# Token-mixed rows transposed by sixteen SBUF-to-SBUF copies and VectorE blocks instead of TensorE, with scores two units ahead

## Chip, cores and metric

One core of one Trainium2 chip. The metric is the device time of one execution in microseconds (us), median of several. Profiles are of one execution each; where the record gives both, its span is 1.7 to 1.9 us shorter than its time. An *issue* below is the time that an engine's queue (SyncE's is `SPq`) is occupied with starting one DMA; a DMA *lands* when its data have arrived. SBUF is the memory of the kernel's tiles, PSUM that of the matmuls' results.

## The reference

Eight batches of pooled-key attention, then an MLP mixer on the result; all inputs and the output are float32, the kernel computes in bfloat16.

```python
# q, k, v: (8, 8, 576, 64); keys and values averaged over groups of 8 -> 72 keys
attn = softmax(q @ k_pooled^T / 8)            # per batch and head
x  = (attn @ v_pooled) as (batch, 576, 512)
h  = relu(x^T @ w_tok1) @ w_tok2              # token mixing: 576 -> 256 -> 576
u  = x + h^T
out = u + relu(u @ w_ch1) @ w_ch2             # channel MLP: 512 -> 1536 -> 512
```

The channel MLP's first matmul sums over the 512 channels, so `u`, made with tokens on the partitions, is needed transposed (`uT`, channels on the partitions).

## The kernel before

A *unit* is one batch's channel MLP: 48 matmuls of 512 columns in a first stage (w_ch1) and 48 in a second (w_ch2). Between them, at numbered steps (two matmuls each), stand the attention and token mixing of the next batch. The order on TensorE, GpSimd, VectorE (DVE) and ScalarE (ACT) is the order in which the program issues; the timelines keep to it (in unit 3 of the changed kernel VectorE stands 11.17 us before a block transpose, with a q block and a kD copy of 0.27 us behind it). The transpose and the schedule, cut:

```python
def uT(c):                                     # 4 TensorE transposes, then one VectorE copy from PSUM
    def go():
        src = st["u"][:, c, :] if c < 4 else u_tails[:, b // 2, :]
        ...
        for kk in range(4):
            nc.tensor.transpose(out=ps[:, kk, :], in_=src[:, kk * P:(kk + 1) * P], identity=ident)
        nc.vector.tensor_copy(out=dst[:, :, o:o + P], in_=ps)
...
TAIL = {23: "av0", 25: "av1", 27: "av2", 29: "av3", 31: "av4", 33: "at0", 34: "at1",
        37: "u0", 38: "u1", 39: "t0", 40: "u2", 41: "t1", 42: "u3", 43: "u4 t2", 45: "t3", 47: "t4"}
LATER = {0: "kpT", 3: "s0", 6: "P0", 8: "s1", 11: "P1", 13: "s2", 16: "P2", 18: "s3", 20: "P3", **TAIL}
```

`kpT` transposes the pooled keys (into `kD`), `Q`/`P` are VectorE's block transposes of q (into `qD`), `s` scores, `av` attention times values, `at` and `u` the token mixing, `t` the transposes of u. The last 64 of a batch's 576 rows go, two batches together, through a ninth unit (`u4`, `t4`, "tails").

The softmax here doesn't subtract the row's maximum and nothing guards it: scores larger than these inputs give would overflow.

## Time and profile before

| | before |
|---|---|
| time, median | 290.4 us (3 runs) |
| span of the profile | 290.8 us (of an execution of 292.6 us) |
| TensorE busy | 95% |
| VectorE / ScalarE / GpSimd busy | 52% / 33% / 45% |
| mean granted TensorE clock | 0.994 |
| TensorE holes over 0.5 us after the start-up | unit 0 and its end only, but for two of 0.6 us at unit boundaries |

"Busy" counts overlapping matmuls once, so I read TensorE by the distances of its starts: 216 ns for 512 columns. A *hole* below is the distance of two neighbouring starts less that pace. The lines are in the prediction.

### The profile page before, as it was taken

To read this page: it belongs to the slowest core of one execution; us is meant where nothing else is said; L and a number is where in the kernel's file an instruction comes from. 1 tells how busy PE (TensorE), PEld (TensorE's weight loads), DVE (VectorE), ACT (ScalarE), POOL (GpSimd) and SP (SyncE) were. 2 spreads that over 40 slices of the span, in tenths; PEclk is the share of its full clock that TensorE was granted. 3 is DMA by queue.
4 is the path that set the end of the run, shared out by engine and by line. 5 is a ranking of instruction groups with operands and counts; after the bars stand their busy time and mean duration, and the time that the engine had idled before them with its cause. 6 is when DMAs were issued, how large, how long until landed. Compare 5 with 4: busy or idle time off the path is not lost.

```text
span 290.8 us, 4636 instructions
## 1 busy us (share of the span) xinstructions
PE 276.8 (95%) x1876; PEld 137.9 (47%) x1912; DVE 151.3 (52%) x304; ACT 95.6 (33%) x173; POOL 130.1 (45%) x121
## 2 busy tenths in 40 slices
PE   7989989989999999999999999999999999999994
PEld 3755456433455445443544454445443545444443
DVE  5465814695377436754755476637551656121122
ACT  2544682004800470037103710173027200511500
POOL 8593103999999979940999934000000000000000
PEclk9999999997999999999999999999999999999999
DMA  7999999948829839552843011300320031114014
GB/s 150 194 205 205 204 195 187 229 82 132 152 42 158 191 39 177 111 86 61 146 92 72 2 32 42 72 0 2 72 60 14 2 73 41 34 36 102 6 38 108
DMA packets 25157, 27.97 MB, mean 96 GB/s; under 512 B 4656, under 2 KB 18864, under 8 KB 25136
## 3 DMA queue, kind: packets, MB, share of 16 engines
q0 software_dynamic: 18928, 17.64, 39.1%
q1 hardware_dynamic: 6048, 9.90, 14.1%
q8 instruction: 15, 0.25, 0.3%
q10 hardware_dynamic: 160, 0.13, 0.2%
q14 instruction: 6, 0.05, 0.1%
HBM read 35.85 MB, written 9.44 MB: 156 GB/s over the span
## 4 chain that ended last, share of the span: by engine, by line
PE 77%; POOL 10%; DVE 6%; ACT 2%; DMA 2%; issue 2%; POOLq 0%
PE p L473 26%; PE p L447 26%; PE p L387 5%; PE p L372 5%; POOL t L154 4%; PE p L326 3%; POOL t L155 3%; PE p L288 2%; PE pt L397 2%; DMA kr<-in_k_dram 2%; PE p L254 1%; PE p L306 1%; POOL kp L158 1%; DVE qD L277 1%; PE p L462 1%
## 5 line engine op out<-in xcount | busy, mean ns | idle before, releaser
L473 PE MATMUL p<-w_ch,GT 128*128 128x512 bf16 x401 | 105.8, 379 | 0.6
L447 PE MATMUL p<-uT,w_ch 128*128 128x512 bf16 x372 | 91.1, 383 | 0.9 <-issue 0.5
L452 ACT ACTIVATE GT<-p 128x512 bf16<-128x512 f32 x84 | 48.7, 596 | 108.2 <-PE p L447 95.9
L447 PEld LDWEIGHTS <-w_ch 128*128 128x128 bf16 x432 | 39.8, 98 | 47.2 <-issue 6.6
L473 PEld LDWEIGHTS <-GT 128*128 128x128 bf16 x420 | 37.5, 98 | 33.6 <-issue 0.2
L454 DVE TENSOR_SCALAR GT<-p 128x512 bf16<-128x512 f32 x24 | 16.6, 692 | 63.8 <-PE p L447 63.8
L155 POOL TENSOR_TENSOR t<-t 72x512 f32<-72x512 f32 x24 | 30.3, 1261 | 1.9
L294 ACT ACTIVATE ex<-p 72x576 bf16<-72x576 f32 x48 | 28.3, 640 | 6.6 <-PE p L288 6.6
L478 DVE TENSOR_TENSOR o<-p,u 128x512 f32<-128x512 f32 x32 | 22.0, 687 | 10.4 <-PE p L473 10.2
L388 DVE TENSOR_TENSOR u<-p,x 128x512 bf16<-128x512 f32 x32 | 22.1, 690 | 9.0 <-PE p L387 9.0
L154 POOL TENSOR_TENSOR t<-kr 72x1024 f32<-72x1024 bf16 x12 | 25.5, 2125 | 0.1
L154 POOL TENSOR_TENSOR t<-vr 72x1024 f32<-72x1024 bf16 x12 | 25.4, 2119 | 0.0
L363 ACT ACTIVATE AT<-p 128x512 bf16<-128x512 f32 x8 | 4.8, 597 | 52.8 <-PE p L372 50.1
L344 DVE TENSOR_TENSOR x<-p,den 128x512 bf16<-128x512 f32 x30 | 20.7, 692 | 1.0
L326 PEld LDWEIGHTS <-ex 72*128 72x128 bf16 x320 | 15.4, 98 | 9.9 <-DVE x L344 0.8
L387 PE MATMUL p<-AT,w_tok 128*128 128x512 bf16 x64 | 19.0, 379 | 0.1
L277 DVE STREAM_TRANSPOSE qD<-qb 128x576 bf16<-128x576 bf16 x24 | 18.7, 805 | 0.0
L326 PE MATMUL p<-vp,ex 72*128 72x65 bf16 x320 | 16.8, 194 | 0.9 <-DVE x L344 0.6
L365 DVE TENSOR_SCALAR AT<-p 128x512 bf16<-128x512 f32 x8 | 5.5, 692 | 17.3 <-PE p L372 16.5
L372 PE MATMUL p<-x,w_tok 128*128 128x512 bf16 x56 | 14.4, 379 | 0.1
L398 DVE COPY uT<-pt 128x512 bf16<-128x512 bf16 x28 | 11.8, 420 | 3.4 <-PE pt L397 3.4
L118 POOL DMA_DIRECT2D qb<-in_q_dram x6 | 4.3, 722 | 18.8 <-DVE qD L277 12.3
(93 smaller groups left out, 236.6 us busy)
## 6 DMA issues: line engine op xcount, KB each, us to landing
out_dram<-o SPq DMA_DIRECT2D x70, 128.0 KB, 2.4
kr<-in_k_dram POOLq DMA_DIRECT2D x7, 576.0 KB, 8.3
qb<-in_q_dram POOLq DMA_DIRECT2D x7, 576.0 KB, 10.5
vr<-in_v_dram POOLq DMA_DIRECT2D x7, 576.0 KB, 14.2
w_ch<-in_moe_w_ch_dram POOLq DMA_DIRECT2D x6, 512.0 KB, 12.8
qf<-in_q_dram SPq DMA_DIRECT2D x2, 288.0 KB, 3.0
kr<-in_k_dram POOLq DMA_DIRECT2D x2, 256.0 KB, 6.3
vr<-in_v_dram POOLq DMA_DIRECT2D x2, 256.0 KB, 7.6
```

The source lines that it names most:

```text
L154: eng.tensor_tensor(out=t4[:, 0:n], in0=t[:, hs, 0:4], in1=t[:, hs, 4:8], op=ALU.add)
L155: eng.tensor_tensor(out=t4[:, 0:n, 0:2], in0=t4[:, 0:n, 0:2], in1=t4[:, 0:n, 2:4], op=ALU.add)
L277: nc.vector.transpose(out=st["qD"][:, g, db].rearrange("m (r j u) -> m u r j", u=2, r=BR), in_=st["qraw"][:, g].rearrange("m (u r d) -> m ...
L294: nc.scalar.activation(out=exv[:, h:h + 2], in_=pss[a][0:SP, :, 0:SH], func=AF.Exp, scale=scale)
L326: nc.tensor.matmul(out=halves[h // 4][:, (h % 4) * (D + 1):(h % 4 + 1) * (D + 1)], lhsT=st["ex"][:, h * S + n0:h * S + n0 + P], rhs=st["vp ...
L372: nc.tensor.matmul(out=ps, lhsT=w_tok1[:, c if c < 4 else 4 + par, m * P:(m + 1) * P], rhs=st["x"][:, c, :] if c < 4 else st["xt"], start= ...
L387: nc.tensor.matmul(out=ps, lhsT=w, rhs=a, start=(i == 0), stop=(i == len(mms) - 1))
L388: nc.vector.tensor_tensor(out=dst, in0=ps, in1=x, op=ALU.add)
L447: nc.tensor.matmul(out=ps, lhsT=w_ch1[:, kk, m * P:(m + 1) * P], rhs=uT[:, kk, :], start=(kk == 0), stop=(kk == 3))
L452: nc.scalar.activation(out=GT[:, m, :], in_=ps, func=AF.Relu)
L473: nc.tensor.matmul(out=ps, lhsT=GT[:, m, c * P:(c + 1) * P], rhs=w_ch2[:, m, :], start=(m == 0), stop=(m == NM - 1))
L478: nc.vector.tensor_tensor(out=o_sb, in0=ps, in1=u_all[:, c, :], op=ALU.add)
```

## The change

The intent is to take the transposes of u off TensorE for batches 2 to 7. A 128x128 transpose is put together from sixteen copies, each of which moves a 32-partition quadrant to another quadrant, and from VectorE's transposes, which the program takes to work within blocks of 32x32. So that the score phase does not compete with ScalarE's activations in the first stage, scores are computed two batches ahead, in the second stage, and ScalarE takes all activations. w_ch1's rows are permuted to match. Batch 1 loses its special path.

```diff
+        def shuffle(part, src):
+            def go():
+                st[part] = swap.tile([P, 4 if part == "v" else 1, DM], BF16, name=part)
+                for a in range(4):
+                    for i in range(4):
+                        nc.sync.dma_start(out=st[part][32 * a:32 * a + 32, :, i * P:(i + 1) * P],
+                                          in_=src()[32 * i:32 * i + 32, :, a * P:(a + 1) * P])
...
+        def blocks(c):
+            def go():
...
+                nc.vector.transpose(out=dst[:, :, o:o + P].rearrange("f k (a t) -> f a k t", a=4),
+                                    in_=src.rearrange("t (a f k) -> t a k f", a=4, k=4))
...
-            if m % 4 != 3 or n == 0:
-                nc.scalar.activation(out=GT[:, m, :], in_=ps, func=AF.Relu)
-            else:
-                nc.vector.tensor_scalar(out=GT[:, m, :], in0=ps, scalar1=0.0, scalar2=None, op0=ALU.max)
+            nc.scalar.activation(out=GT[:, m, :], in_=ps, func=AF.Relu)
...
-    LATER = {0: "kpT", 3: "s0", 6: "P0", 8: "s1", 11: "P1", 13: "s2", 16: "P2", 18: "s3", 20: "P3", **TAIL}
+    FIRST = {0: "K0 V0", 1: "<u0", 2: "<u1", 4: "<u2", 6: "<u3 k1", 8: "Q0", 10: "Q1", 12: "kpT Q2", 14: "Q3 v1",
...
+    SECOND = {0: "s0 V0 V1 L >K0 >K1 >V0 >V1", 3: "s1", 6: "s2", 9: "s3", 13: "av0", 15: "av1", 17: "av2", 19: "av3", 21: "av4",
+              23: "at0 >Q0", 24: "at1", 27: "u0", 28: "u1", 30: "u2", 31: "u3 M", 33: "u4 M4 >Q1 >kpT", 34: "T0",
+              35: ">Q2", 36: "T1 >s0", 37: ">Q3", 38: "T2", 39: ">s1", 40: "T3", 42: "T4 >s2", 45: ">s3"}
+    LATER = {0: ">K0 >K1 L >V0 >V1 av0", 2: "av1", 4: "av2", 6: "av3", 8: "av4", 10: "at0 >Q0", 11: "at1",
+             14: "u0", 15: "u1", 17: "u2", 18: "u3 M", 20: "u4 M4 >Q1", 21: "T0", 22: "T1", 24: ">Q2 >kpT",
+             25: "T2", 27: ">Q3 >s0", 29: "T3", 31: "T4 >s1", 35: ">s2", 39: ">s3"}
```

`M` is the sixteen copies (`M4` those of the tails), `T` a block transpose, `>` marks work for the batch two ahead, `L` the loads of a batch three ahead, `K`/`V` GpSimd's pooling, `k`/`v` VectorE's. FIRST is unit 0, SECOND unit 1, LATER all others.

## The prediction

What no trace of this case shows is cut out of the recorded text, and the cuts are marked. After the first of them "what that is" means the issue of a DMA, after the second "such a VectorE operation" is a block transpose. One term of the sum is cut: +0.4 us for batch 1's scores in part 2. The trace before does not show it: there 16 score matmuls of the old form hold TensorE 2.0 us, 32 of the new form 1.5 us. The net of 2.5 us contains that term (without it 2.9), and the sum stands: 290.4 - 6.0 - 2.5 - 2 = 279.9 us, with 57.6 us of holes and 10.2 us of slow stretches 348 us, from which 341 us was chosen. A slow stretch of 1.7 us at each hole was the estimate, from the start-up's eight matmuls in 3.59 us.

> **What bounds the kernel now.** I read the busy table first, then the chain that ended last, then the costliest groups, then stretches of the timeline.
>
> ```profile
> PE 276.8 (95%) x1876; PEld 137.9 (47%) x1912; DVE 151.3 (52%) x304; ACT 95.6 (33%) x173; POOL 130.1 (45%) x121
> ...
> PE   7989989989999999999999999999999999999994
> ...
> PE 77%; POOL 10%; DVE 6%; ACT 2%; DMA 2%; issue 2%; POOLq 0%
> ```
>
> TensorE is busy 95% of the span, at 9 in nearly every slice, and the chain of waits runs on it for 77%. So the program is a queue of matmuls without holes, and a change pays only by what it takes out of that queue, or costs what it puts holes into it. The cadence of the queue is seen in the PE timeline of a stretch in the middle:
>
> ```profile
> 150.32 0.39 PE L397 MATMUL pt<-ident,u 128*128 128x128 bf16 x4
> 150.54 0.59 PE L473 MATMUL p<-w_ch,GT 128*128 128x512 bf16 x2
> 150.98 0.59 PE L387 MATMUL p<-AT,w_tok 128*128 128x512 bf16 x2
> ```
>
> The durations overlap (the matmuls are pipelined), so I take the distances of the starts: four transposes hold the queue 0.22 us (56 ns each), two 512-column matmuls 0.44 us (216 ns each). The groups name what the change removes:
>
> ```profile
> L397 PE MATMUL pt<-ident,u 128*128 128x128 bf16 x112 | 10.8, 219 | 0.2
> ...
> L397 PE MATMUL pt<-ident,u_tails 128*128 128x128 bf16 x16 | 1.5, 219 | 0.5 <-DVE uT L398 0.5
> ```
>
> 128 transposes look like 12.3 us of busy time there, but at 56 ns each they hold the queue only 7.2 us. The only real holes lie in the first batch's unit and at its end, in the PE timeline there:
>
> ```profile
> 63.64 0.38 PE L397 MATMUL pt<-ident,u_tails 128*128 128x128 bf16 x4 [0.46 <-DVE uT L398]
> ...
> 65.93 0.29 PE L215 MATMUL pt<-ident,kp 72*128 72x72 bf16 x4 [1.48 <-DVE uT_tails L398]
> ...
> 66.71 1.91 PE L447 MATMUL p<-uT,w_ch 128*128 128x512 bf16 x4 [0.22 <-issue]
> ```
>
> After that hole of some 1.5 us, four matmuls take 1.91 us, twice their usual pace. A hole costs itself and then a slow stretch. At the program's start (the PE timeline's first line) eight go in 3.59 us before the fast pace begins; against 8 x 216 ns = 1.7 us, some 1.7 us are lost.
>
> [...] The trace shows what that is in time, in SyncE's own timeline of two stretches:
>
> ```profile
> 0.74 0.86 SPq L108 DMA_DIRECT2D qf<-in_q_dram  x2
> ...
> 112.63 1.11 SPq L481 DMA_DIRECT2D out_dram<-o  x2
> ```
>
> that is 0.43 and 0.56 us per issue. [...] The trace has such a VectorE operation for q:
>
> ```profile
> L277 DVE STREAM_TRANSPOSE qD<-qb 128x576 bf16<-128x576 bf16 x24 | 18.7, 805 | 0.0
> ...
> L388 DVE TENSOR_TENSOR u<-p,x 128x512 bf16<-128x512 f32 x32 | 22.1, 690 | 9.0 <-PE p L387 9.0
> ...
> out_dram<-o SPq DMA_DIRECT2D x70, 128.0 KB, 2.4
> ```
>
> **The change, part by part.** A "unit" is one batch's channel MLP with the attention of later batches between its matmuls.
>
> 1. Removed from TensorE: of the 128 transposes of u, the built program keeps 20 (batch 1). 108 x 56 ns = 6.0 us, all on the path.
> 2. Batch 1 loses 20 q transposes (1.1 us), half of its v pooling on TensorE (16 matmuls of 256 columns, 109 ns apart, 1.7 us) and four small k transposes (0.1 us)[...]. Net 2.5 us.
> 3. Batch 1's pooling, before wholly a VectorE chain of some 5 us on which TensorE waits, is split with GpSimd. I allow 2 us for smaller holes in the first two units.
> 4. ScalarE takes all hidden activations (24 more of 596 ns) and the scores move to the second stage. ScalarE is 33% busy, so this costs nothing.
> 5. Added: for each of six batches, sixteen SBUF-to-SBUF DMAs of 32 KB, all issued by SyncE, then four VectorE block transposes; for odd batches sixteen further DMAs of 8 KB for the tail rows. VectorE loses the copies from PSUM (420 ns) and gets 512-element block transposes, estimated 805 x 512/576 = 0.72 us; with 52% busy that is affordable.
>
> Parts 1 to 3: 290.4 - 6.0 - 2.5 - 2 = 279.9 us without new holes.
>
> **Where part 5 puts holes.** I read the order of the built program. In units 2 to 5 TensorE has, between the last matmul of u3 (which the copies wait for) and the first score matmul of the batch two ahead, 18 matmuls of 216 ns and four small k transposes: 4.0 us, or 4.9 us in even units with the four tail matmuls. VectorE has in its queue: u3, one q block, first block transpose (waits for all sixteen copies), second one, another q block, and only then the copy of the k transposes that those scores need. So the scores wait for the copies, although they use nothing of them. The chain from the end of u3's matmul:
>
> - u3's addition with its latency: 0.9 us (0.69 + 0.2)
> - sixteen issues at 0.56 us: 8.9 us
> - landing of the last: 2.4 us from issue to landing, less its own issue: 1.8 us
> - two block transposes, a q block, the k copy (286 ns), latencies: 0.72 + 0.72 + 0.81 + 0.29 + 0.2 = 2.7 us
>
> Sum 14.3 us, so TensorE stands still 14.3 - 4.0 = 10.3 us in units 3 and 5 and 9.4 us in units 2 and 4. Unit 1 copies later, but its third score waits behind the first block transpose: 11.6 us to landing, plus 3.7 us of VectorE work, less 6.0 us of matmuls up to there, is 9.5 us with latency. Unit 6 has no scores ahead, but the tail's block transpose waits for 32 issues (20.5 us), and the additions that free the PSUM buffers stand behind it: 22.1 us against 13.4 us of matmuls, 8.7 us. Total 2 x 10.3 + 2 x 9.4 + 9.5 + 8.7 = 57.6 us. Each such hole is far longer than the one at 64 us, so each brings a slow stretch of 1.7 us, 6 x 1.7 = 10 us. 279.9 + 57.6 + 10.2 = 348 us.
>
> If an issue costs 0.37 to 0.43 us, as the cheapest here, the copies are done 2 to 3 us earlier in each unit (twice that in unit 6): about 18 to 22 us less, some 327 us. I choose 341 us between the two, nearer the trace's mean of SyncE issues.
>
> **The rivals.**
>
> (a) The copies are hidden: transfers of 32 KB are small, the DMA engines are little busy in the second half (shares of 0 to 4 tenths), and uT is needed only a full second stage later. Then the time is about 280 us, 3.6% faster. For it: the author set the block transposes only three steps (1.3 us of matmuls) after the copies, as somebody who thinks them quick. Against it: the measured 0.43 to 0.56 us per issue, sixteen in a row on one sequencer, and the order of VectorE's queue. It would need an issue of about 0.1 us.
>
> (b) The transfers are slower than I take them. Copies of 256-byte rows have no example in this trace, and while GpSimd's loads run, the output stores land later: in the first 130 us several take about 6 us instead of 2.4. There are eight semaphores for SyncE's DMAs in the built order, so every ninth issue waits for a landing; at 6 us each the sixteen would take two rounds, 12 us or more. That gives another 2 to 5 us per unit, 355 to 370 us.
>
> (c) The new bound is VectorE or ScalarE by sheer work. Against it: 52% and 33% busy before, and the change adds some 8 us to VectorE and 14 us to ScalarE while it takes 17 us of activations from VectorE. It would make nothing of the time by itself.
>
> **Range and chances.** Low end: cheap issues and little slow-down of the clock, 280 + 35 = 315. High end: rival (b) in part, 366. The mechanism must hold for "slower": one SyncE sequencer, about half a microsecond per issue, and strict order on VectorE. I give it 0.89. Rival (a) has 0.08, and a balance within 2% has 0.03.
>
> **What would show the steps right or wrong.** Right: TensorE's busy share falls to about 80%; in its row of slices one dent per unit from about 90 us on; the waits list TensorE's score group waiting on VectorE's kD copy or qD block some 9 us, four or five times; VectorE's block transpose waits for the DMA of v; SyncE's timeline has sixteen issues in 7 to 10 us after each u3; the mean granted clock falls below 0.97. L397's successor has 20 instructions, and matmul cadence outside the dents is still 216 ns. Wrong: sixteen issues in under 3 us, or a first block transpose that starts before TensorE reaches the scores; then the time is near 280 us. If the holes are there but the copies take 15 us or more, the landing was mis-sized and the time is above the range.

## The result

| | before | after |
|---|---|---|
| time, median (range) | 290.68 us (290.42 to 292.26, 4 runs) | 366.98 us (365.36 to 369.27, 4 runs) |
| ratio | | 1.262, 95% interval 1.254 to 1.269 |
| profile's span | 290.8 us | 364.3 us |
| mean granted clock | 0.994 | 0.902 |

Ratios here and below are the mean time of one kernel's runs over the mean of the other's of the same rounds, so not quite the ratio of the medians. The result is correct and 26% slower.

The page of the changed kernel: busy, TensorE's row of slices, its clock, the chain that ended last, and SyncE's new issues:

```profile
PE 285.7 (78%) x1780; PEld 130.9 (36%) x1780; DVE 146.9 (40%) x276; ACT 110.3 (30%) x193; POOL 139.4 (38%) x127
...
PE   7996599999519952999079962999089994599995
...
PEclk9999699999957995999769995999769998689999
...
PE 59%; SPq 17%; DMA 9%; DVE 9%; issue 2%; POOL 2%; ACT 0%; DVEq 0%; POOLq 0%
...
v<-u SPq DMA_DIRECT2D x96, 32.0 KB, 1.9
```

There is one dent per unit, at each the clock falls, and SyncE's queue ("SPq") has entered the chain with 17%. One copy lands 1.9 us after its issue begins (median); what takes long is that there are sixteen in a row. The waits of the whole program (who waited for whom, total, times, longest) put names on the dents:

```profile
...
DVE uT L386 <- DMA v<-u: 65.7, 6, 13.4
DVE o L466 <- PE p L461: 63.5, 21, 14.5
POOL qb L114 <- DVE qD L249: 53.2, 4, 21.6
PEld L260 <- DVE kD L202: 44.3, 4, 11.5
PE p L260 <- DVE kD L202: 42.3, 4, 11.0
```

VectorE waits six times for the copies, once per unit 1 to 6, and TensorE's scores (L260) wait four times 10 to 11 us for a VectorE copy of 0.27 us (kD). Unit 3 in the timelines of SyncE, VectorE and TensorE:

```profile
170.52 10.35 SPq L378 DMA_DIRECT2D v<-u  x16
...
169.80 0.69 DVE L360 TENSOR_TENSOR u<-p,x 128x512 bf16<-128x512 f32 x1 [0.17 <-PE p L359]
170.41 0.81 DVE L249 STREAM_TRANSPOSE qD<-qb 128x576 bf16<-128x576 bf16 x1
182.39 1.30 DVE L386 STREAM_TRANSPOSE uT<-v 128x512 bf16<-128x512 bf16 x2 [11.17 <-DMA v<-u]
183.62 0.78 DVE L249 STREAM_TRANSPOSE qD<-qb 128x576 bf16<-128x576 bf16 x1
184.30 0.27 DVE L202 COPY kD<-pt 128x288 bf16<-128x288 bf16 x1
...
172.33 1.46 PE L461 MATMUL p<-w_ch,GT 128*128 128x512 bf16 x6
184.62 0.70 PE L260 MATMUL p<-qD,kD 32*72 32x288 bf16 x8 [10.83 <-DVE kD L202]
185.25 3.36 PE L461 MATMUL p<-w_ch,GT 128*128 128x512 bf16 x8
```

Read from the top: u is ready at 170.5; sixteen issues take 10.35 us (0.65 each); VectorE stands before the first block transpose until 182.39; only behind the second does it reach the q block and the kD copy that the scores wait for; TensorE stands still from 173.6 to 184.6 and then runs eight matmuls in 3.36 us, half pace.

**Where 73.5 us of span come from.** Holes in units 1 to 6: 64.9 us (table in the part on why the prediction was wrong). Slow stretches, counted as two or more neighbouring 512-column matmuls whose starts lie 0.36 to 0.50 us apart, in excess of 0.216 (a single such distance can be a record missing from the trace): 14.0 us against 2.3, so +11.7. Unit 0 and its end: holes over 0.5 us of 7.9 us against 3.7, so +4.2. That makes 80.8; the 7.3 us between are what is left for the work removed (8.5 by the prediction, parts 1 and 2) and for all that is smaller than these counts.

### The profile page after: what moved, and what is told of

The parts are those of the page before. It is cut to its first block, busy times and chain, and to the rows that moved or that the text cites. A ratio compares the mean times of both kernels' runs of the same rounds, so it can differ in the third digit from the quotient of the medians.

```text
span 364.3 us, 4570 instructions
## 1 busy us (share of the span) xinstructions
PE 285.7 (78%) x1780; PEld 130.9 (36%) x1780; DVE 146.9 (40%) x276; ACT 110.3 (30%) x193; POOL 139.4 (38%) x127
## 4 chain that ended last, share of the span: by engine, by line
PE 59%; SPq 17%; DMA 9%; DVE 9%; issue 2%; POOL 2%; ACT 0%; DVEq 0%; POOLq 0%
PE p L438 23%; PE p L461 18%; SPq L378 17%; DMA v<-u 6%; PE p L344 4%; PE p L359 4%; PE p L260 3%; PE p L298 3%; DMA vt<-u_tails 2%; DVE qD L249 2%; DMA kr<-in_k_dram 2%; DVE u L360 2%; DVE uT L386 1%; DVE t L150 1%; PE p L450 1%
## 5 line engine op out<-in xcount | busy, mean ns | idle before, releaser
L461 PE MATMUL p<-w_ch,GT 128*128 128x512 bf16 x420 | 109.7, 407 | 4.6 <-DVE o L466 4.6
L438 PE MATMUL p<-uT,w_ch 128*128 128x512 bf16 x384 | 101.1, 392 | 4.8 <-DVE o L466 4.8
L442 ACT ACTIVATE GT<-p 128x512 bf16<-128x512 f32 x108 | 64.2, 597 | 108.1 <-PE p L438 108.1
L266 ACT ACTIVATE ex<-p 72x576 bf16<-72x576 f32 x56 | 33.2, 643 | 106.4 <-PE p L260 106.4
L461 PEld LDWEIGHTS <-GT 128*128 128x128 bf16 x420 | 40.6, 103 | 57.6 <-issue 19.8
L260 PE MATMUL p<-qD,kD 32*72 32x288 bf16 x224 | 15.3, 333 | 54.4 <-DVE kD L202 42.3
L386 DVE STREAM_TRANSPOSE uT<-v 128x512 bf16<-128x512 bf16 x24 | 15.9, 687 | 65.7 <-DMA v<-u 65.7
L151 POOL TENSOR_TENSOR t<-t 72x512 f32<-72x512 f32 x26 | 33.7, 1295 | 2.1
L260 PEld LDWEIGHTS <-kD 32*72 32x72 bf16 x224 | 5.1, 116 | 69.6 <-DVE kD L202 44.3
L114 POOL DMA_DIRECT2D qb<-in_q_dram x7 | 5.0, 719 | 58.8 <-DVE qD L249 53.2
L249 DVE STREAM_TRANSPOSE qD<-qb 128x576 bf16<-128x576 bf16 x28 | 22.1, 795 | 0.1
L310 DVE RECIPROCAL den<-p 128x8 f32<-128x8 f32 (+1 forms) x39 | 8.0, 205 | 18.8 <-PE p L298 18.6
## 6 DMA issues: line engine op xcount, KB each, us to landing
vr<-in_v_dram POOLq DMA_DIRECT2D x7, 576.0 KB, 11.9
```

What stands on the lines that cost most here:

```text
L151: eng.tensor_tensor(out=t4[:, 0:n, 0:2], in0=t4[:, 0:n, 0:2], in1=t4[:, 0:n, 2:4], op=ALU.add)
L249: nc.vector.transpose(out=late("qD")[:, g, db].rearrange("m (r j u) -> m u r j", u=2, r=BR), in_=st["qraw"][:, g].rearrange("m (u r d) -> ...
L260: nc.tensor.matmul(out=pss[l // 2][0:SP, l % 2, 0:SH], lhsT=st["kD"][quad, g, db, :], rhs=st["qD"][quad, g, db, half * SH:(half + 1) * SH] ...
L266: nc.scalar.activation(out=exv[:, h:h + 2], in_=pss[a][0:SP, :, 0:SH], func=AF.Exp, scale=scale)
L438: nc.tensor.matmul(out=ps, lhsT=w_ch1[:, kk, m * P:(m + 1) * P], rhs=uT[:, kk, :], start=(kk == 0), stop=(kk == 3))
L442: nc.scalar.activation(out=GT[:, m, :], in_=ps, func=AF.Relu)
```

## Experiments

The theory: TensorE's scores stand behind VectorE's block transposes in VectorE's queue, these behind sixteen issues on SyncE, and every long hole also costs a slow stretch. Rivals: the bytes or the loads beside them set the time; the move of the scores itself costs; the slow clock is no consequence of the holes. Nine kernels ran, each once profiled, on chips with runs of the kernel before beside them (medians of before 290.9, 291.2 and 292.5 us in the three groups). All deltas below are against the changed kernel's 367.0 us if not said otherwise; it did not run again beside these groups.

### Sixteen issues, a quarter of the bytes (wrong result)

```diff
-  nc.sync.dma_start(out=st[part][32*a:32*a+32, :, i*P:(i+1)*P], in_=src()[32*i:32*i+32, :, a*P:(a+1)*P])
+  nc.sync.dma_start(out=st[part][32*a:32*a+32, 0:1, i*P:(i+1)*P], in_=src()[32*i:32*i+32, 0:1, a*P:(a+1)*P])
-  src = st["v"][:, c, :] if c < 4 else ...
+  src = (st["u"][:, c, :] if c else st["v"][:, c, :]) if c < 4 else ...
```

> Wrong result on purpose: each of the sixteen copies moves one chunk of u instead of four (8 KB instead of 32 KB); three of the four block transposes read u itself, though still in VectorE's queue behind the first. Number and order of issues as in the changed kernel. Theory (sixteen issues one after the other on SyncE, 0.64 us apart, set the hole): the span from the first issue to the last landing stays near 12 us, TensorE's holes stay at 10 to 11 us, and the time is within 2% of the changed kernel's 367 us. Rival (moving 256-byte rows is what takes long, or the loads beside it): the copies fall to a third or so, the holes shrink by 5 us or more each, and the time falls below 340 us.

347.02 us (2 runs), ratio to before 1.192 [1.184, 1.200]. Unit 3's timelines of SyncE and VectorE:

```profile
162.56 10.05 SPq L378 DMA_DIRECT2D v<-u  x16
...
174.10 0.71 DVE L386 STREAM_TRANSPOSE uT<-v 128x512 bf16<-128x512 bf16 x1 [7.73 <-DMA v<-u]
```

From the first issue to the block transpose: 11.5 us against 11.9 us with four times the bytes. So the issues set the length, as the theory has it. But the expected time was missed by 20 us: copying chunk 0 alone needs only u0, so the copies started 3.1 us earlier relative to the scores (at u0's end instead of u3's), and the holes of units 2 to 5 shrank from 9.9 to 11.2 us to 6.4 to 7.6 us. I had overlooked that dependency; the experiment is read by the length of the copy phase, not by the time.

### Four issues, the same bytes (wrong result)

```diff
-                for a in range(4):
-                    for i in range(4):
-                        nc.sync.dma_start(out=st[part][32*a:32*a+32, :, i*P:(i+1)*P], in_=src()[32*i:32*i+32, :, a*P:(a+1)*P])
+                for a in range(4):
+                    i = (a + 1) % 4
+                    nc.sync.dma_start(out=st[part][:, :, i*P:(i+1)*P], in_=src()[:, :, a*P:(a+1)*P])
```

> Wrong result on purpose: the same bytes in the same 256-byte rows, but in four issues over all 128 partitions instead of sixteen over 32. Theory (issues): twelve issues at 0.64 us fall away, 7.7 us of each hole, so that holes of 3 to 4 us stay in units 1 to 5 and none or little in unit 6 (there 24 issues fall away); with five shorter holes and a shorter slow stretch the time is 315 to 330 us. Rival (bytes): holes and time as in the changed kernel, 360 us or more.

315.42 us (2 runs), ratio 1.083 [1.074, 1.092]: -51.6 us. Unit 3 again, SyncE, VectorE, TensorE:

```profile
157.65 2.73 SPq L378 DMA_DIRECT2D v<-u  x4
...
162.13 1.30 DVE L385 STREAM_TRANSPOSE uT<-v 128x512 bf16<-128x512 bf16 x2 [3.78 <-DMA v<-u]
...
164.36 0.44 PE L260 MATMUL p<-qD,kD 32*72 32x288 bf16 x8 [3.45 <-DVE kD L202]
```

The same 512 KB in the same 256-byte rows are there 4.5 us after the first issue. Twelve issues fewer took 7.4 us off unit 3's hole. The number of issues is shown as the main cause, the bytes are not. Unit 2 kept a hole of 6.9 us: there a load of k ran beside the four copies, and they landed 8.6 us after the first issue instead of 4.4.

### The scores first: block transposes at the end of the second stage

```diff
     LATER = {..., 10: "at0 >Q0", 11: "at1",
+             12: "<T4",
-             14: "u0", 15: "u1", 17: "u2", 18: "u3 M", 20: "u4 M4 >Q1", 21: "T0", 22: "T1", 24: ">Q2 >kpT",
-             25: "T2", 27: ">Q3 >s0", 29: "T3", 31: "T4 >s1", 35: ">s2", 39: ">s3"}
+             14: "u0", 15: "u1", 17: "u2", 18: "u3 M", 20: "u4 M4 >Q1", 24: ">Q2 >kpT",
+             27: ">Q3 >s0", 31: ">s1", 35: ">s2", 39: ">s3", 42: "T0", 43: "T1", 44: "T2", 45: "T3"}
```

> Right result. Only the order of VectorE's queue in units 2 to 7 is changed: the block transposes stand after everything that the scores ahead need, at the end of the second stage, and the tail's in the next unit. The copies themselves are untouched. Theory (the scores wait for copies that they do not use): the holes of units 2 to 6 (about 52 us together) and their slow stretches (about 12 us) go, a short wait of up to 1 us at each unit's end may come; unit 1 keeps its hole. Time 300 to 310 us. Rival (the copies are simply too late for the next unit, wherever VectorE waits for them): the hole moves to the start of the next unit and the time stays above 345 us.

320.94 us (4 runs), ratio 1.103 [1.098, 1.108], correct: -46 us by order alone. No score in units 2 to 5 waits for the copies any more; unit 1, left as it was, keeps its 12.3 us. The time is 11 us above the expected range, because the ends of units 2 and 3 now wait 6.4 and 5.0 us (units 4 to 6: 0.75 to 2.5 us). TensorE and SyncE in unit 2:

```profile
147.33 1.01 PE L438 MATMUL p<-uT,w_ch 128*128 128x512 bf16 x2 [6.26 <-DVE uT L386]
...
126.32 12.51 SPq L378 DMA_DIRECT2D v<-u  x16
```

There the last copy landed 18.4 us after the first issue, in unit 3 16.0 us, in units 4 to 6 11.7 to 12.3 us (unit 1, beside a load of k, 13.8). In just these two units GpSimd's loads of the next q and v were in flight; GpSimd's timeline in unit 2:

```profile
130.69 0.72 POOL L114 DMA_DIRECT2D qb<-in_q_dram  x1 [4.22 <-DVE qD L249]
```

The cause is in the order: the load of q waits for VectorE's last q block of the batch two before (the 53.2 us of the wait list above), and moving the block transposes back let that block, and hence the loads, start in the midst of the copies. That is rival (b) of the prediction, which the next run tests.

### The same without loads (wrong result)

```diff
+        if b >= 4:
+            loaded[b] = loaded[b - 2]      # batches 4 to 7 read the inputs of 2 and 3 again
+            return
```

> Wrong result on purpose: the run with the scores first (320.9 us), but batches 4 to 7 read the inputs of batches 2 and 3 again, so that no load runs beside the copies from unit 1 on. There the sixteen copies took 18.4 and 16.0 us from first issue to last landing in units 2 and 3, where loads ran, and 11.7 to 12.3 us in units 4 to 6, and TensorE waited 6.4 and 5.0 us at the ends of units 2 and 3. Theory (loads in flight hold the copies back): 11.5 to 12.5 us in every unit, the waits at the ends of units 2 and 3 fall to some 1 us as in units 4 and 5, the hole of unit 1 shrinks by about 2 us, and with two slow stretches less the time falls by 10 to 14 us, to 307 to 311 us. Rival (units 2 and 3 are slow for another reason, such as the order of GpSimd's work): copies and waits as before, 318 us or more.

306.46 us (2 runs), ratio 1.050 [1.038, 1.062] to a median of 292.46 before. Unit 2, TensorE and SyncE:

```profile
142.26 0.59 PE L441 MATMUL p<-uT,w_ch 128*128 128x512 bf16 x2 [0.59 <-DVE uT L389]
...
126.93 10.34 SPq L381 DMA_DIRECT2D v<-u  x16
```

All copies now land 11.7 to 12.4 us after the first issue, the waits at the ends of units 2 and 3 are 0.75 and 1.3 us, and the time fell by 14.5 us, to just below the expected range. Unit 1's hole shrank by 1.4 us. So loads in flight do hold the copies back, shown by taking them away. Why (sharing of the DMA engines, or of something behind them) is not settled.

### TensorE transposes, everything else of the change kept

```diff
-    ... 18: "u3 M", 20: "u4 M4 >Q1", 21: "T0", 22: "T1", ...   (and so in SECOND)
+    ... 18: "u3", 20: "u4 >Q1", 21: "t0", 22: "t1", ...
```

> Right result. The changed kernel with its schedule two units ahead, its load order and ScalarE's activations, but u is transposed by TensorE as before, at the places of the block transposes; no copies. Theory: no holes but those of the first two units (some 7 us in unit 0 against 2 to 3 us before, as the trace of the changed kernel shows), 6.0 us of transposes come back; 290.4 - 2.5 (batch 1's work) + 4 to 5 = 291 to 294 us, within 2% of the kernel before. Rival (moving the scores two units ahead costs time by itself, by PSUM buffers or ScalarE): above 300 us.

296.75 us (4 runs), ratio 1.019 [1.014, 1.023], correct. That is 3 us above the expected range. The copies and their waits are worth 70 us of the 76; scores two units ahead, as such, cost nothing visible. What stays is unit 0, with 7.7 us of holes over 0.5 us, where the kernel before has 1.4 us (and 2.3 more at the unit's end), and a slow stretch of 1.5 us behind them:

```profile
34.80 0.24 PE L200 MATMUL pt<-ident,kp 72*128 72x72 bf16 x2 [1.91 <-POOL kp L154]
40.48 0.30 PE L200 MATMUL pt<-ident,kp 72*128 72x72 bf16 x2 [5.45 <-DVE kp L154]
```

### The holes filled with spare matmuls

```diff
+                if s == "F":                                  # "F" stands before ">s0" (unit 1: ">s2")
+                    if n + 2 < B:
+                        ps = ps_two.tile([P, 2, 512], FP32, name="p2")
+                        for _ in range(44):
+                            nc.tensor.matmul(out=ps[:, 0], lhsT=warm[:, 0:P], rhs=warm, start=True, stop=True)
...
```

> Right result. The changed kernel with 44 spare matmuls of 512 columns (44 x 216 ns = 9.5 us) ahead of the scores at which TensorE stands still, once in each of units 1 to 5. They need nothing and fit into the holes of 9.9 to 12.5 us, so the wait itself is untouched; only the array does not stand idle. Theory (each hole also costs a slow stretch of 1.4 to 1.7 us, five of the six here): no slow stretch after these holes, mean granted clock from 0.90 up to 0.96 or more, and the time falls by 6 to 9 us, to 358 to 361 us, although work was added. Rival (the slow stretches have another cause, or the spare matmuls delay the scores): the time stays at 367 us or rises.

361.43 us (2 runs), ratio 1.240 [1.234, 1.247], correct: 5.6 us less time with 220 matmuls more. Unit 3, TensorE:

```profile
175.63 9.66 PE L508 MATMUL p<-warm 128*128 128x512 bf16 x44
186.80 0.44 PE L260 MATMUL p<-qD,kD 32*72 32x288 bf16 x8 [1.51 <-DVE kD L202]
187.40 1.67 PE L461 MATMUL p<-w_ch,GT 128*128 128x512 bf16 x7 [0.16 <-issue]
```

The wait ends when it did, but the seven matmuls behind it run at full pace (1.67 us; eight took 3.36 us before). The clock rose from 0.902 to 0.967 and the slow stretches fell from 14.0 to 8.5 us; those left are the start-up's, units 0 and 6, where nothing was filled, and short ones in units 1 and 2. The slow stretches are a consequence of the holes, but not of their length alone. In all traces here a hole of 4 us or more has one behind it (in the changed kernel seven to twelve 512-column matmuls, 1.4 to 2.5 us lost); below that both happen. With four issues, holes of 3.6 and 3.7 us (units 3 and 5) have full pace behind them and one of 2.8 us (unit 4) a slow stretch, and so has the 1.6 us hole at the end of unit 0 in the kernel before. As to the expectation, the gain is at the lower edge of what I expected.

### A scratch buffer of its own for VectorE's pooling (on the variant with TensorE transposes)

```diff
-        t4 = att.tile([SP, H // 2, 4, D], FP32, name="t4")
+        t4 = (swap.tile([SP, H // 2, 4, D], FP32, name="t4v") if eng is nc.vector else
+              att.tile([SP, H // 2, 4, D], FP32, name="t4"))
```

> Right result. The variant that transposes by TensorE throughout, and VectorE's pooling of batch 1 gets a scratch buffer of its own. In the changed kernel and in that variant it waited 3.3 us for the buffer that GpSimd's pooling still held, and then ran beside GpSimd's next pooling at 3.1 us instead of 1.2 us for its first step. Theory 1 (the buffer is the cause of unit 0's hole of some 7 us): VectorE starts 3.3 us earlier, the hole shrinks to 3 to 4 us, and the time falls from 296.7 to 292 to 294 us. Theory 2 (running beside GpSimd is the cause): it starts earlier but takes as long or longer, and the time stays above 295 us.

292.62 us (4 runs), ratio 1.003 [0.999, 1.007], correct: 4.1 us less than the variant without. In the changed kernel VectorE's pooling of batch 1 (timeline):

```profile
34.38 3.13 DVE L150 TENSOR_TENSOR t<-kr 72x1024 f32<-72x1024 bf16 x1 [3.30 <-POOL kp L154]
37.55 1.63 DVE L151 TENSOR_TENSOR t<-t 72x512 f32<-72x512 f32 x1
```

With its own buffer:

```profile
30.35 1.21 DVE L151 TENSOR_TENSOR t4v<-kr 72x1024 f32<-72x1024 bf16 x1
31.59 2.52 DVE L152 TENSOR_TENSOR t4v<-t4v 72x512 f32<-72x512 f32 x1
```

VectorE starts 4 us earlier: the pool of two scratch buffers was the wait. But its steps still take long: beside GpSimd's pooling its first step took up to 3.1 us instead of 1.2, its second up to 2.5 instead of 0.7, and in the changed kernel GpSimd's own second step took 2.1 us instead of 1.25. Both theories have a part. The hole shrank to 4.0 and 0.8 us and is now GpSimd's pooling, which is as late.

### Batch 1's keys pooled by TensorE (on the variant with TensorE transposes)

```diff
+        def kpool_pe(g):            # 8 matmuls with the identity, summed in PSUM, one VectorE copy into kp
...
-    FIRST = {0: "K0 V0", ..., 6: "<u3 k1", 8: "Q0", 10: "Q1", ...
+    FIRST = {0: "V0", ..., 6: "<u3", 7: "x0", 8: "Q0", 9: "x1", 10: "Q1", ...
-    LATER: 22: "t1", 25: "t2", 31: "t4 >s1"
+    LATER: 23: "t1", 26: "t2", 31: ">s1", 33: "t4"
```

> Right result. TensorE transposes throughout, scores two units ahead, and batch 1's keys are pooled by TensorE (16 matmuls of 256 columns, 109 ns apart, 1.7 us) so that neither VectorE nor GpSimd is waited for in unit 0; in the even units one transpose each is set a little later, where 0.87 us were lost. Theory: the hole of 7.7 us and its slow stretch of 1.5 us go, 1.7 us of matmuls come: 296.7 - 7.7 - 1.5 - 1.5 + 1.7 = 287.7 us, so 286 to 290 us, about 1% faster than the kernel before. Rival (the keys of batch 1 arrive too late for whoever pools them): a hole of 3 us or more stays, above 291 us.

288.09 us (6 runs), ratio 0.9885 [0.9855, 0.9915], correct, granted clock 1.0. No hole of 0.6 us or more is left in units 0 to 8. So the schedule two units ahead, with batch 1's work removed and its keys pooled by TensorE, is 1.1% faster than the kernel before; what each of the three gives was not tested. The 1.1% is against two kinds of runs of that kernel together, seven of 290.3 to 291.2 us at a clock of 1.0 and four of 292.2 to 292.4 us at 0.994; against the first kind alone it is 0.9%.

### The same, with copies for batches 5 and 6 only

```diff
+    COPIED = {... 18: "u3 M", 20: "u4 >Q1", 24: ">Q2 >kpT", 27: ">Q3 >s0", 29: "t4", 31: ">s1", 35: ">s2", 39: ">s3",
+              42: "T0", 43: "T1", 44: "T2", 45: "T3"}
-            unit(n, LATER)
+            unit(n, COPIED if n in (4, 5) else LATER)
```

> Right result. The same kernel, but batches 5 and 6, in whose units no loads run, are transposed by the copies and VectorE, with the block transposes at the end of the second stage as in the run with the scores first; the tails stay with TensorE. Theory: 32 transposes of 56 ns fall away, 1.8 us, and up to 1 us per unit is lost where the next unit waits for the last block transpose: 0 to 1.8 us faster than the kernel with TensorE throughout, 0.6% at most, 285 to 289 us. Rival (the copies disturb even here): slower than it by 2 us or more.

286.75 us (5 runs), ratio 0.9844 [0.9814, 0.9874], correct: the best of all, 1.6% below the kernel before, and 0.4% (of the two ratios) below the one with TensorE throughout. In units without loads, behind the scores, and without the tails' copies, the copies are hidden but for an idle time of 0.6 us at the unit's end, 0.75 us by the distance of starts (TensorE's timeline; unit 5's end looks the same):

```profile
182.37 0.59 PE L450 MATMUL p<-uT,w_ch 128*128 128x512 bf16 x2 [0.59 <-DVE uT L397]
```

## Why the prediction was wrong

It had direction and mechanism: "the scores wait for the copies, although they use nothing of them", shown by the reordering (-46 us) and by the four issues (-52 us). The steps that failed are sizes: the row of sixteen issues (8.9 us in the sum, 10.3 to 11.8 measured, longest beside loads), the 2 us gain in the first two units, and the way from the sum's 348 us down to 341. Measured were 367 us, 1 us above the range; forecast +51 us, measured +76. Of the 26 us between 341 and 367, the choice makes 7, the holes 7.3 (3.0 of them in unit 1, 1.8 in unit 2), unit 0 6.2, the slow stretches 1.5; of the other 4, 1 is less work removed than counted and 3 that the profile of the kernel before is of one of its longer executions.

| hole in unit | predicted | measured |
|---|---|---|
| 1 | 9.5 | 12.5 |
| 2 | 9.4 | 11.2 |
| 3 | 10.3 | 11.0 |
| 4 | 9.4 | 9.9 |
| 5 | 10.3 | 10.9 |
| 6 | 8.7 | 9.4 |
| sum, us | 57.6 | 64.9 |

Unit 6's came in two, 4.8 us behind the block transposes and 4.6 us behind the tail's.

- **Sixteen issues at 0.56 us: mis-sized.** In unit 3 the terms of the chain were 0.8 us to the first issue (predicted 0.9), 10.35 us of issues (8.9), 1.5 us to the first block transpose (1.8), 2.2 us of VectorE work (2.7); 14.9 us in all (14.3). I had averaged pairs of stores; a copy's issue takes longer, also alone (lines below the list). My lower variant of 0.37 to 0.43 us was further off still: the cheapest SyncE issue in the trace before took 0.39 us, and seven times 2 to 3 us are 15 to 21 us, not "18 to 22".
- **Landings beside loads: left to a rival.** In units 1 and 2 a load of k ran beside the copies and they took 14.0 and 12.9 us to the last landing instead of 11.7 to 12.1; these are the units most over the prediction. Rival (b) named it, and its 355 to 370 us held the time, but by luck: it priced 2 to 5 us in every unit, where two units lost 2.3 and 1.2 us, and its wait of every ninth issue for a landing (the built program has eight semaphores for SyncE's DMAs) came to 2.0 us in the whole program, 1.07 of them before the ninth copy of unit 2. The run without loads shows the effect.
- **Unit 0: wrong in sign.** "I allow 2 us for smaller holes" as a gain; the holes of unit 0 and its end grew by 4.2 us. I counted VectorE's and GpSimd's pooling as independent. They shared two scratch buffers (VectorE waited 3.30 us for one), and steps that ran side by side took longer (VectorE's first 3.1 us instead of 1.2). A pool's count of buffers is in the source, and I had not read it for that.
- **Slow stretches: right.** Predicted 10.2 us, measured +11.7, unit 0's 1.5 included; 1.4 to 1.5 us in each of units 1 to 5, 4.1 in unit 6. The filled holes show the cause.
- **Work removed: not measured alone.** The account above leaves 7.3 us for it and for small things, predicted 8.5. 20 of 128 transposes were left; with TensorE transposing again and unit 0 mended, the schedule gave 288.1 us. The prediction's 279.9 us "without new holes" was never reached, since it included the transposes of six batches hidden for nothing and unit 0's gain.
- **The choice of 341 instead of 348: wrong way.** My own sum said 348. I moved it down for an issue cheaper than the trace's mean, which the pairs of stores (0.47 and 0.60 us) spoke against.
- **Rival (a)** (hidden copies) fell in this kernel. In the last experiment, for two of the six batches, with another order and no loads beside them, the copies were hidden but for 0.6 us. **Rival (c)** (VectorE or ScalarE as bound) fell: 40% and 30% busy.

The issues, by SyncE's timelines. In the kernel before, the two loads of q took 0.39 and 0.42 us, the first store of a pair took 0.47 us, the second 0.60:

```profile
112.63 0.47 SPq L481 DMA_DIRECT2D out_dram<-o  x1
...
113.14 0.60 SPq L481 DMA_DIRECT2D out_dram<-o  x1
```

In a row of copies nearly all took 0.60 us, with 0.04 us of gap. It looks as if the first of a pair were cheap because it finds an idle queue. But the first copy of a row, after 12.4 us without an issue, took 0.64 us (unit 4 of the changed kernel; 0.64 to 0.73 in the six units):

```profile
211.19 0.64 SPq L378 DMA_DIRECT2D v<-u  x1
```

So a copy of 32 KB is no cheaper at the head of the row (one of 8 KB is, by 0.04 us), and why a store is, by 0.13 us, stays open. No DMA in the trace before was such a copy; that the second store's 0.60 us fits may be chance.

## What to carry to other kernels

Count DMA issues, not bytes, when a transfer is cut in many pieces: multiply the issue's time, measured on such a transfer if possible (here 0.64 us from copy to copy, where I had taken 0.56 from stores), and ask what stands behind the wait in the same engine's queue. Put a consumer of late data behind everything in that queue that others need sooner (-46 us here), and look then at what this releases: here it let loads start in the midst of the copies, whose last landing came 16.0 and 18.4 us after the first issue instead of 11.7 to 12.3. A hole of 4 us or more in TensorE cost a further 1.4 to 2.5 us of half pace in the changed kernel; shorter ones did so only sometimes. Not tried: sharing the sixteen issues between SyncE's queue and another engine's.
